# One core: where the row scales are fetched, and the order of loads and scalings between block 0 and block 1 of a layer norm, state-space and Mish kernel

## The chip, the cores and the metric

The kernel runs on one core of a Trainium2 chip. Its time is the device time of one execution in microseconds. A profile is one execution recorded by the hardware profiler; its span runs from the first to the last instruction.

## The reference

x is 2048 rows of 1024 numbers (bf16). It is normalised by rows, and two branches of the normalised rows are added to x:

```
xn  = layernorm(x)
B_bar = ((exp(dt*Lambda) - 1) / Lambda)[:, None] * (B_re + 1j*B_im)
Bu  = xn @ B_bar.T                       # 1024 complex states
h_t = exp(dt*Lambda) * h_(t-1) + Bu_t    # along the 2048 rows
A   = 2 * real(h @ C.T) + xn * Dskip
hh  = xn @ w1 + b1                       # 1024 -> 3584
B   = (hh * tanh(softplus(hh))) @ w2     # Mish, 3584 -> 1024
out = x + A + B
```

## The kernel before, in words

**Blocks.** The rows are worked in four blocks of 512. For each block the kernel computes w1 and Mish (28 tiles of 128 columns, `first_tile`), the projection into the states (B), the recurrence on VectorE (`recur`, state chunks j = 0 to 7), the product with w2 (`dense`) and the projection out of the states (C), which adds up in the same PSUM banks as w2; `finish` then adds the banks to x, and `store` writes x out on ScalarE's queue. Block 0 uses plain products. From block 1 on, the product with B and most of that with w1 are done in a fast form: seven products of half size per 2 by 2 partition (numbers 1 to 7), for which sums and differences of the factors are needed, in f16. For that the factors must first be scaled by powers of two.

**What is prepared during block 0's tail for block 1.** (1) *B*: `rows_load(i)` reads 16 row chunks of B (eight buffers within `act`, given by `row_slot`) on GpSimd's queue; `rows_size(i)` on ScalarE sums their absolute values and at its end issues load i + 8; `rows_scale(h)` on VectorE makes the scales of half h (states 0 to 511 for h = 0, from sizes 0 to 7) and stores them as a row to DRAM (`scd`); `rows_fetch(h)` reads that row back, spread over 128 partitions, to act buffer 18 + h; `rows_spread(h)` puts it in order and `scale_B` multiplies B by it on VectorE. (2) *w1*: seven groups of 512 columns. `w_load(i)` reads a group raw, four DMAs on GpSimd's queue (group 3 to hb buffers 8 to 15, group 4 to hb 0 to 7, group 5 to act 20 to 27); `w_scale(i)` scales it on ScalarE, two instructions, and stores three quarters of it (`wsd`) on GpSimd's queue; `w_sums(i)` makes the four sums on VectorE and stores these. SyncE's ring loads bring the stored units back as they are used. (3) *C*: `scale_C(j)` scales C on ScalarE and VectorE with scratch in hb 0 to 7; `keep_C(j)` stores it on ScalarE's queue.

**What sets the order.** Each engine works its instructions in the order in which the program emits them, its DMA issues among them; there is no planner. An instruction waits by semaphores for the last writer of what it reads, and for the last writer and all readers of what it writes; a buffer that is only named among the writes orders instructions in the same way:

```python
        waits = _hazards(reads, writes, ev)
        self.items.append((fn, waits.values(), dsem.sem, 16))
        _record(reads, writes, ev)
```

PSUM has eight banks; block 1's tiles 0 to 11 use bank f % 8, and a bank is free again when ScalarE's Mish of its tile has read it. Block 0's last additions (`finish`, q = 0 to 3) free banks 0 and 1, then 2 and 3, and so on. Block 0's w2 items are used in the order 0 to 8, 13, 9 to 12 (item g covers act buffers 2g and 2g + 1), so buffers 18 and 19 are read by the eleventh item and 20 and 21 by the twelfth.

At the start of block 1 (`side(0)`), VectorE makes the sums of B (`sums_B`) and of x (`sums_x`, written over block 0's x, once that is stored), then the sums of groups 3 and 4. Block 1's products (L952 with B, L1024 with w1) follow in the order written in `WHOLE`; `w_load(6)` waits until group 3's hb buffers have been stored.

Of the kernel before, what the change touches and what calls it, by code (L numbers as in the profile page):

```python
# [142 lines left out]
def bass_parallel_sum__ssm_conv_s5__dense_activation_mish__prompt_kernel(  # L143
    nc: bass.Bass,
    A_x: bass.AP,
    A_Lambda_re: bass.AP,
    A_Lambda_im: bass.AP,
    A_B_re: bass.AP,
    A_B_im: bass.AP,
    A_C_re: bass.AP,  # L150
    A_C_im: bass.AP,
    A_log_dt: bass.AP,
    A_Dskip: bass.AP,
    B_x: bass.AP,
    B_w1: bass.AP,
    B_b1: bass.AP,
    B_w2: bass.AP,
    out: bass.AP,
):
    build_kernel(nc, A_x, A_Lambda_re, A_Lambda_im, A_B_re, A_B_im, A_C_re, A_C_im,  # L160
                 A_log_dt, A_Dskip, B_w1, B_b1, B_w2, out)


def build_kernel(nc, A_x, A_Lambda_re, A_Lambda_im, A_B_re, A_B_im, A_C_re, A_C_im,
# [5 lines left out]
    TB = 512  # L170
# [44 lines left out]
    AC = Queue(nc, "ac")  # L215
    PO = Queue(nc, "po")
    SP = Queue(nc, "sp")
# [15 lines left out]
    b_actf = [Buf("act%d" % f, parts=[Buf("act%d_%d" % (f, h)) for h in range(2)]) for f in range(NF)]  # L233
# [45 lines left out]
    def c(n):  # L279
        return cs[:, CN.index(n), :]  # L280
# [28 lines left out]
    srow0 = act[:, 18:20, :].rearrange("p f t -> p (f t)")  # L309
# [9 lines left out]
    def wsm(n, lo, hi):  # L319
        return cs[:, CN.index("den") + n, lo:hi]  # L320
# [759 lines left out]
    def w_unit(where):  # L1080
        kind, t = where
        v = hb if kind == "h" else act
        return v[:, t:t + 2, :].rearrange("p f t -> p (f t)"), (b_hbf if kind == "h" else b_actf)[t:t + 2]
# [3 lines left out]
    def w_raw(i, ci, kh):  # L1087
        kind, t = W_RAW[i]
        return kind, t + 2 * (2 * ci + kh)

    def w_load(i):
        sem = DmaSem(nc, "d_wraw%d" % i, nper=4)
        for ci in range(2):
            for kh in range(2):
                dst, b_dst = w_unit(w_raw(i, ci, kh))
                f0 = (4 * i + 2 * ci) * P
                src = B_w1[kh * NH * P:(kh + 1) * NH * P, f0:f0 + 2 * P].rearrange("(k p) f -> p k f", p=P)
                PO.dma(lambda e, dst=dst, src=src: e.dma_start(dst.rearrange("p (k f) -> p k f", k=NH), src),
                       sem, writes=b_dst)

    def w_half(i, ci):
        kind, t = w_raw(i, ci, 0)
        v, b_v = (hb, b_hbf) if kind == "h" else (act, b_actf)
        return v[:, t:t + 4, :].rearrange("p f t -> p (f t)"), b_v[t:t + 4]
# [53 lines left out]
    def w_store(i, n, t, b_t):  # L1158
        PO.dma(lambda e: e.dma_start(wsd[i][n - 1], t), DmaSem(nc, "d_wsd%d_%d" % (i, n)),  # L1159
               reads=b_t, writes=[b_wsd[i][n - 1]])  # L1160

    def w_scale(i, cis=(0, 1)):
        for ci in cis:
            t, b_t = w_half(i, ci)
            aop(lambda e, t=t: e.activation(t, t, AF.Copy, scale=wsm(2, i, i + 1)),  # L1165
                reads=b_t + [b_wsm[2][i]], writes=b_t)
        for n, ci, kh in ((1, 0, 0), (2, 0, 1), (4, 1, 1)):
            if ci in cis:
                w_store(i, n, *w_unit(w_raw(i, ci, kh)))
# [288 lines left out]
    def carry(queue=VE):  # L1458

        hl = hT[:, :, :, TB - 1]  # L1460
        for s, n in enumerate(("c1", "s1")):
            for ci in range(2):
                o = qi[:, ci, :] if s == 0 else qt[:, ci, :]
                queue.op(lambda e, o=o, n=n, ci=ci: e.tensor_tensor(o, hl[:, ci, :], c(n), op=ALU.mult),
                    reads=b_hT[ci] + [b_cs[n]], writes=[b_qi if s == 0 else b_qt[ci]])
        queue.op(lambda e: e.tensor_tensor(qi[:, 0, :], qi[:, 0, :], qt[:, 1, :], op=ALU.subtract),
            reads=[b_qi, b_qt[1]], writes=[b_qi])
        queue.op(lambda e: e.tensor_tensor(qi[:, 1, :], qi[:, 1, :], qt[:, 0, :], op=ALU.add),
            reads=[b_qi, b_qt[0]], writes=[b_qi])
# [253 lines left out]
    NHS = 8  # L1723
# [3 lines left out]
    def row_slot(i):  # L1727
        f0 = (12, 0, 2, 4, 6, 8, 10, 14)[i % NHS]
        return act[:, f0:f0 + 2, :].rearrange("p f t -> p (f t)"), b_actf[f0:f0 + 2]

    def rows_load(i):
        j, ci = i // 2, i % 2
        t, b_t = row_slot(i)
        if NHS // 2 <= i < NHS:
            b_t = b_t + [b_actf[19]]
        PO.dma(lambda e: e.dma_start(t, (A_B_re, A_B_im)[ci][j * P:(j + 1) * P, :]), s_nat[i % NHS], writes=b_t)

    def rows_size(i):
        j, ci = i // 2, i % 2
        t, b_t = row_slot(i)  # L1740
        aop(lambda e: e.activation(t, t, AF.Abs, scale=2.0, accum_out=cj("ab%d" % ci, j)), reads=b_t,  # L1741
            writes=b_t + [b_ab[ci][j // 4]])
        if i + NHS < 2 * NJ:
            rows_load(i + NHS)

    def rows_scale(h):
        hs = slice(NJ // 2 * h, NJ // 2 * (h + 1))
        ab0, ab1, ss, si = (c(n)[:, hs] for n in ("ab0", "ab1", "ss", "si"))
        e8, f8 = si_i[:, 0, hs], si_i[:, 1, hs]
        b_a, b_e, b_f = b_ab[0][h], b_si_i[0][h], b_si_i[1][h]  # L1750

        def power(o, b_o, src, b_s, m, a):
            vop(lambda e: e.tensor_scalar(f8, src, m, a, op0=ALU.mult, op1=ALU.add), reads=[b_s], writes=[b_f])
            vop(lambda e: e.tensor_scalar(o.bitcast(i32), f8, 23, None, op0=ALU.logical_shift_left), reads=[b_f], writes=[b_o])

        vop(lambda e: e.tensor_tensor(ab0, ab0, ab1, op=ALU.add), reads=[b_a, b_ab[1][h]], writes=[b_a])
        vop(lambda e: e.tensor_scalar(ab0, ab0, 2.0 ** 100, 2.0 ** -100, op0=ALU.min, op1=ALU.max),
            reads=[b_a], writes=[b_a])
        vop(lambda e: e.tensor_scalar(e8, ab0.bitcast(i32), 24, None, op0=ALU.logical_shift_right),
            reads=[b_a], writes=[b_e])  # L1760
        power(ss, b_ss[h], e8, b_e, -2.0, 2.0 * 127 + 9)
        vop(lambda e: e.tensor_copy(sbf[:, hs], ss), reads=[b_ss[h]], writes=[b_sbf[h]])
        power(si, b_si[h], e8, b_e, 1.0, 59.0)
        power(ab1, b_ab[1][h], e8, b_e, -1.0, 195.0)
        (AC if h else PO).dma(lambda e: e.dma_start(scd[h], sbf[:, hs]), DmaSem(nc, "d_scd%d" % h),
                              reads=[b_sbf[h]], writes=[b_scd[h]])

    def rows_fetch(h):
        (AC if h else PO).dma(lambda e: e.dma_start(srow0[:, TB * h:TB * (h + 1)],
                                     scd[h].rearrange("p j -> (p j)").partition_broadcast(P)),  # L1770
               DmaSem(nc, "d_srow%d" % h), reads=[b_scd[h]], writes=[b_actf[18 + h]])

    def rows_spread(h):
        vop(lambda e: e.tensor_copy(srow[:, TB * h:TB * (h + 1)].rearrange("p (j q) -> p j q", q=P),
                                    srow0[:, TB * h:TB * (h + 1)].rearrange("p (q j) -> p j q", q=P)),
            reads=[b_actf[18 + h]], writes=[b_actf[16 + h]])

    def keep_C(j):
        AC.dma(lambda e: e.dma_start(ctd[j], CT[:, j, :, :].rearrange("p c d -> p (c d)")), s_ctd[j],
               reads=[b_CT[j]], writes=[b_ctd[j]])  # L1780
# [5 lines left out]
    def scale_B(pr, cis=(0, 1)):  # L1786
        js = slice(2 * pr, 2 * pr + 2)
        b_B = b_BT[js]
        row = srow[:, 2 * P * pr:2 * P * (pr + 1)].rearrange("p (j q) -> p j q", j=2)
        for ci in cis:  # L1790
            vop(lambda e, ci=ci: e.tensor_tensor(
                BT[:, ci, js, :, :], BT[:, ci, js, :, :], row.unsqueeze(2).to_broadcast([P, 2, NK, P]), op=ALU.mult),
                reads=b_B + [b_actf[16 + pr // 2]], writes=b_B)
# [29 lines left out]
    for blk in range(NB):  # L1823
# [67 lines left out]
        for j in range(NJ):  # L1891
# [49 lines left out]
            if j == 3:  # L1941
                for i in range(NHS):
                    rows_load(i)
# [15 lines left out]
                w_sums(i, True)  # L1959
        if blk == FAST - 1:  # L1960
            keep_C(NJ - 1)
            w_load(4)
            w_load(5)
            rows_scale(1)
            for n in ("c1", "s1"):
                PO.op(lambda e, n=n: e.tensor_tensor(c(n), c(n), c("ab1"), op=ALU.mult), reads=[b_cs[n]] + b_ab[1], writes=[b_cs[n]])
            carry(PO)
            rows_fetch(1)
        for _ in out_stage:
            pass  # L1970
        if blk == FAST - 1:
            w_scale(3)
            w_scale(4)
            rows_spread(0)
            scale_B(0)
            scale_B(1, (0,))
# [36 lines left out]
```

## Time and profile before

| | us |
|---|---|
| three runs | 597.64, 598.75, 594.12 |
| median | 597.64 |
| profiled execution: time | 599.66 |
| profiled execution: span | 598.4 |
| busy: TensorE / VectorE / ScalarE / GpSimd | 587.6 / 504.8 / 402.8 / 156.4 |

The profile's lines name engine, source line and operation, and the tiles as out<-in. In a timeline a row gives start and duration in us, the number of instructions merged in it, and in brackets the idle time of the engine before it with what ended it. A q behind an engine's name is its sequencer, which issues DMAs. In a table of stages each engine's busy time and number of instructions are followed by the granted TensorE clock (1.00 is full), the share of the DMA engines' time, and GB/s. Matmuls overlap: 128 x 512 ones start 0.216 us apart, though each is drawn with 0.38 us.

### The profile page before, as it was taken

To read this page: it belongs to the slowest core of one execution; us is meant where nothing else is said; L and a number is where in the kernel's file an instruction comes from. 1 tells how busy PE (TensorE), PEld (TensorE's weight loads), DVE (VectorE), ACT (ScalarE), POOL (GpSimd) and SP (SyncE) were. 2 spreads that over 40 slices of the span, in tenths; PEclk is the share of its full clock that TensorE was granted. 3 is DMA by queue.
4 is the path that set the end of the run, shared out by engine and by line. 5 is a ranking of instruction groups with operands and counts; after the bars stand their busy time and mean duration, and the time that the engine had idled before them with its cause. 6 is when DMAs were issued, how large, how long until landed. Compare 5 with 4: busy or idle time off the path is not lost.

```text
span 598.4 us, 9801 instructions
## 1 busy us (share of the span) xinstructions
PE 587.6 (98%) x3643; PEld 355.2 (59%) x3643; DVE 504.8 (84%) x759; ACT 402.8 (67%) x540; POOL 156.4 (26%) x221
## 2 busy tenths in 40 slices
PE   9999999999887999999999999999999999999998
PEld 8644444444333888544448888744446888854444
DVE  6998896997697868999765869899999468789995
ACT  4879981765649977899805677889621798893330
POOL 2899300103645421341210321011510013100000
PEclk9999999999997999999999999999999999999999
DMA  8999999998688989798969967979995956989831
GB/s 252 292 231 244 153 191 213 271 384 286 184 267 297 348 304 332 268 326 236 271 244 403 338 214 254 300 242 276 315 334 187 392 183 219 339 319 321 294 125 70
DMA packets 115785, 160.32 MB, mean 268 GB/s; under 512 B 56074, under 2 KB 67082, under 8 KB 115738
## 3 DMA queue, kind: packets, MB, share of 16 engines
q1 hardware_dynamic: 97696, 105.99, 59.9%
q0 software_dynamic: 13520, 44.19, 23.0%
q10 hardware_dynamic: 4522, 9.52, 4.3%
q8 instruction: 29, 0.48, 0.3%
q14 instruction: 18, 0.15, 0.1%
HBM read 113.52 MB, written 34.08 MB: 247 GB/s over the span
## 4 chain that ended last, share of the span: by engine, by line
PE 88%; DMA 6%; ACT 3%; DVE 2%; issue 1%; ACTq 0%; DVEq 0%; POOLq 0%
PE ps L1484 33%; PE ps L1024 17%; PE ps L952 12%; PE ps L1543 9%; PE ps L875 8%; PE ps L1420 5%; DMA act<-in_A_B_im_dram 2%; DMA ring<-wsd 2%; DMA act<-in_A_B_re_dram 2%; ACT hb L1165 1%; PE ps L684 1%; PE ps L693 1%; ACT act L1741 1%; DVE xx L1683 1%; PE ps L646 1%
## 5 line engine op out<-in xcount | busy, mean ns | idle before, releaser
L1484 PE MATMUL ps<-ring,act 128*128 128x512 bf16 x608 | 131.9, 379 | 0.0
L1484 PEld LDWEIGHTS ps<-ring,act 128*128 128x128 bf16 x608 | 59.5, 98 | 71.3
L1044 ACT ACTIVATE snaps<-ps,par,cs 128x256 f32<-128x256 f32 x98 | 53.4, 563 | 58.2 <-PE ps L1024 36.0
L1484 PE MATMUL ps<-ring,hT 128*128 128x512 bf16 x362 | 78.6, 379 | 0.0
L1024 PE MATMUL ps<-TT,ring 128*128 128x256 f16 x576 | 71.1, 273 | 0.1
L914 DVE TENSOR_TENSOR mt<-hT,tab 128x2048 bf16<-128x2048 bf16 (+1 forms) x56 | 67.9, 1213 | 0.4
L875 PE MATMUL ps<-xnT,ring 128*128 128x512 bf16 x264 | 59.8, 389 | 7.5 <-ACT act L883 5.6
L1024 PEld LDWEIGHTS ps<-TT,ring 128*128 128x128 f16 (+1 forms) x576 | 56.1, 98 | 7.8 <-DMA ring<-wsd 0.3
L1484 PEld LDWEIGHTS ps<-ring,hT 128*128 128x128 bf16 x362 | 35.4, 98 | 42.8
L1435 DVE TENSOR_TENSOR_SCAN hT<-cs,qi,hT 128x512 bf16<-128x512 f32 x48 | 60.7, 1275 | 0.0
L1061 DVE SCALAR_TENSOR_TENSOR act<-ps,cs,snaps 128x512 bf16<-128x512 f32 x54 | 39.8, 748 | 18.8 <-PE ps L1024 16.7
L1024 PE MATMUL ps<-xnT,ring 128*128 128x256 bf16 x432 | 54.5, 273 | 0.0
L875 PEld LDWEIGHTS ps<-xnT,ring 128*128 128x128 bf16 x264 | 26.2, 100 | 40.6 <-issue 11.5
L1209 POOL DMA_DIRECT2D w2d<-hb x28 | 20.1, 718 | 97.3 <-ACT hb L1219 53.7
L1024 PEld LDWEIGHTS ps<-xnT,ring 128*128 128x128 bf16 (+1 forms) x432 | 42.3, 98 | 5.3
L977 DVE TENSOR_TENSOR hT<-ps,snaps 128x512 f16<-128x512 f32 x36 | 23.8, 686 | 15.0 <-ACT snaps L969 13.7
L1455 ACT ACTIVATE hT<-hT,wz 128x1024 bf16<-128x1024 bf16 x16 | 17.9, 1144 | 27.4 <-DVE hT L1450 27.4
L898 ACT ACTIVATE act<-act 128x2048 bf16<-128x2048 bf16 (+3 forms) x12 | 32.8, 2756 | 4.7 <-DVE act L1047 4.7
L1159 POOL DMA_DIRECT2D wsd<-hb x35 | 19.0, 546 | 43.9 <-DVE hb L1181 28.0
L1543 PE MATMUL ps<-ring,act 128*128 128x512 bf16 (+1 forms) x132 | 29.8, 379 | 0.0
L1165 ACT ACTIVATE hb<-hb,cs 128x2048 bf16<-128x2048 bf16 x10 | 19.3, 1993 | 13.8 <-DVE SS L1804 13.8
L1420 PE MATMUL ps<-xnT,BT 128*128 128x512 bf16 x128 | 27.8, 379 | 0.0
(236 smaller groups left out, 1056.3 us busy)
## 6 DMA issues: line engine op xcount, KB each, us to landing
ring<-wsd SPq DMA_DIRECT2D x126, 256.0 KB, 5.3
ring<-in_B_w_dram SPq DMA_DIRECT2D x58, 512.0 KB, 5.4
ring<-ctd SPq DMA_DIRECT2D x24, 512.0 KB, 5.6
ring<-w2d SPq DMA_DIRECT2D x24, 512.0 KB, 5.1
wsd<-hb POOLq DMA_DIRECT2D x35, 256.0 KB, 5.0
w2d<-hb POOLq DMA_DIRECT2D x28, 256.0 KB, 5.0
hb<-in_B_w_dram POOLq DMA_DIRECT2D x20, 256.0 KB, 5.3
ctd<-CT ACTq DMA_DIRECT2D x8, 512.0 KB, 5.9
```

Source lines behind the costliest of these rows:

```text
L875: PE.mm(lambda e, k=k, w=w: e.matmul(ps[:, bank, :], lhsT=w, rhs=xnT[:, k, :], start=k == 0, stop=k == NK - 1), reads=[b_ring[s]] + b_xnT, ...
L898: aop(lambda e: e.activation(t, t, AF.Mish), reads=b, writes=b)
L914: vop(lambda e: e.tensor_tensor(mt[:], u.unsqueeze(1).to_broadcast([P, 2, 2, TB]), tab[:, :, j, :].unsqueeze(2).to_broadcast([P, 2, 2, TB] ...
L952: PE.mm(lambda e, w=w, x=x, o=o, begin=begin, end=end: e.matmul(ps[:, bank, o:o + TH], lhsT=w, rhs=x, start=opens and begin, stop=end, ski ...
L1024: PE.mm(lambda e, w=w, x=x, o=o, begin=begin, end=end: e.matmul(ps[:, bank, o:o + TH], lhsT=w, rhs=x, start=opens and begin, stop=end, ski ...
L1044: aop(lambda e, o=o, p=p, j=j: e.activation(o, p, AF.Identity, scale=ig, bias=b1(f0 + j)), reads=[b_ps[b], b_par, b_ig], writes=b_dst)
L1061: vop(lambda e: e.scalar_tensor_tensor(out=dst, in0=bank(b), scalar=ig, in1=src, op0=ALU.mult, op1=ALU.add), reads=[b_ps[b], b_snap[k], b_ ...
L1165: aop(lambda e, t=t: e.activation(t, t, AF.Copy, scale=wsm(2, i, i + 1)), reads=b_t + [b_wsm[2][i]], writes=b_t)
L1420: PE.mm(lambda e, j=j, ci=ci, k=k, bank=bank: e.matmul(ps[:, bank + ci, :], lhsT=BT[:, ci, j, k, :], rhs=xnT[:, k, :], start=k == 0, stop= ...
L1435: vop(lambda e: e.tensor_tensor_scan(out=hT[:, ci, j, :], data0=cj("r", j).to_broadcast([P, TB]), data1=hT[:, ci, j, :], initial=init, op0 ...
L1484: PE.mm(lambda e: e.matmul(ps[:, u, :], lhsT=lhsT, rhs=rhs, start=st_, stop=last, skip_group_check=blk in SPLIT), reads=reads, writes=[b_p ...
L1543: PE.mm(lambda e: e.matmul(ps[:, bank, :], lhsT=lhsT, rhs=rhs, start=st_, stop=end, skip_group_check=True), reads=b_t + [b_ring[s]], write ...
```

## The change

Five edits, all at the end of block 0:

- `rows_load`: before, each of loads 4 to 7 names act buffer 19 among its writes; after, load 4 alone names act buffer 21.
- `rows_fetch`: the fetch of half 0 moves from GpSimd's queue, that of half 1 from ScalarE's, to SyncE's.
- `rows_scale(1)` and `rows_fetch(1)` are emitted ahead of `w_load(4)`.
- `w_load(5)` is emitted after GpSimd's small products and the carry in place of before them.
- `w_scale(3)` is emitted before the rest of block 0's output stage (the last projection, the additions and the x stores) in place of after it.

```diff
     def rows_load(i):
         j, ci = i // 2, i % 2
         t, b_t = row_slot(i)
-        if NHS // 2 <= i < NHS:
-            b_t = b_t + [b_actf[19]]
+        if i == NHS // 2:
+            b_t = b_t + [b_actf[21]]
         PO.dma(lambda e: e.dma_start(t, (A_B_re, A_B_im)[ci][j * P:(j + 1) * P, :]), s_nat[i % NHS], writes=b_t)
...
     def rows_fetch(h):
-        (AC if h else PO).dma(lambda e: e.dma_start(srow0[:, TB * h:TB * (h + 1)],
+        SP.dma(lambda e: e.dma_start(srow0[:, TB * h:TB * (h + 1)],
                                      scd[h].rearrange("p j -> (p j)").partition_broadcast(P)),
                DmaSem(nc, "d_srow%d" % h), reads=[b_scd[h]], writes=[b_actf[18 + h]])
...
         if blk == FAST - 1:
             keep_C(NJ - 1)
+            rows_scale(1)
+            rows_fetch(1)
             w_load(4)
-            w_load(5)
-            rows_scale(1)
             for n in ("c1", "s1"):
                 PO.op(lambda e, n=n: e.tensor_tensor(c(n), c(n), c("ab1"), op=ALU.mult), reads=[b_cs[n]] + b_ab[1], writes=[b_cs[n]])
             carry(PO)
-            rows_fetch(1)
+            w_load(5)
+            w_scale(3)
         for _ in out_stage:
             pass
         if blk == FAST - 1:
-            w_scale(3)
             w_scale(4)
             rows_spread(0)
             scale_B(0)
```

## The prediction

> **What bounds the kernel now.** I read the page first, then TensorE's timeline around the one dip in its row of slices, then the timelines of ScalarE, GpSimd, VectorE and SyncE over the same 60 us, following each wait to what released it.
>
> ```profile
> PE 587.6 (98%) x3643; PEld 355.2 (59%) x3643; DVE 504.8 (84%) x759; ACT 402.8 (67%) x540; POOL 156.4 (26%) x221
> ...
> 145.84 15.49 PE L1484 MATMUL ps<-CT,hT 128*128 128x512 bf16 x71
> 163.15 13.97 PE L875 MATMUL ps<-xnT,ring 128*128 128x512 bf16 x64 [1.83 <-DVE xx L1683]
> 182.75 9.37 PE L875 MATMUL ps<-xnT,ring 128*128 128x512 bf16 x32 [5.63 <-ACT act L883]
> ...
> 163.00:175.50 12.50, 12.35 (x58) 5.65 (x59) 11.45 (x14) 2.57 (x2) 6.42 (x13) 1.00 0.92 281
> 182.70:186.00 3.30, 3.25 (x8) 1.17 (x9) 3.10 (x5) 3.30 (x5) 1.21 (x3) 0.50 0.94 312
> ```
>
> TensorE is busy for 587.6 of 598.4 us, so at most 10.8 us can come from waits; 1.83 + 5.63 = 7.46 us of them stand here, where block 0 ends and block 1 begins. The stages view adds a third loss: the granted clock is 1.00 after the short wait and 0.50 after the long one. At full clock 64 matmuls of this shape take 13.97 us, starting 0.216 us apart, so 32 should take 6.91; they took 9.37. Lost in this place: 1.83 + 5.63 + 2.46 = 9.92 us.
>
> The long wait is for the first Mish of block 1, which must empty PSUM bank 0. ScalarE shows why it is late:
>
> ```profile
> 141.00 1.06 ACT L1741 ACTIVATE act<-act 128x1024 bf16<-128x1024 bf16 x1 [2.86 <-DMA act<-in_A_B_re_dram]
> 147.55 1.06 ACT L1741 ACTIVATE act<-act 128x1024 bf16<-128x1024 bf16 x1 [3.31 <-DMA act<-in_A_B_im_dram]
> ...
> 158.90 0.18 ACT L1741 ACTIVATION_READ_ACCUMULATOR act<-act 128x1 f32 x1
> 160.96 0.33 ACTq L1765 DMA_DIRECT2D scd<-sbf  x1
> 170.17 0.33 ACTq L1769 DMA_DIRECT2D act<-scd  x1
> 170.53 2.35 ACTq L1669 DMA_DIRECT2D out_dram<-xx  x4
> 172.93 7.68 ACT L1165 ACTIVATE hb<-hb,cs 128x2048 bf16<-128x2048 bf16 x4 [13.84 <-DVE SS L1804]
> 180.63 1.28 ACT L883 ACT_TABLE_LOAD   x1
> ```
>
> The 13.84 us are put down to VectorE, but the issue column tells it better: ScalarE's queue issues the store of the second half's row scale at 160.96 and then its fetch (L1769), which cannot go before the store has landed, at 170.17. Everything behind it stands still: four stores of x, four scalings of w1 groups 3 and 4 (7.68 us), the table load, Mish.
>
> GpSimd shows the other half of the story:
>
> ```profile
> 123.89 0.54 POOL L1736 DMA_DIRECT2D act<-in_A_B_re_dram  x1 [11.49 <-PE ps L1484]
> 129.72 0.54 POOL L1736 DMA_DIRECT2D act<-in_A_B_im_dram  x1 [5.29 <-DMA act<-in_A_B_re_dram]
> 136.30 0.54 POOL L1736 DMA_DIRECT2D act<-in_A_B_re_dram  x1 [6.04 <-DMA act<-in_A_B_im_dram]
> 141.26 0.54 POOL L1736 DMA_DIRECT2D act<-in_A_B_im_dram  x1 [4.43 <-DMA act<-in_A_B_re_dram]
> ...
> 150.21 0.55 POOL L1765 DMA_DIRECT2D scd<-sbf  x1 [0.68 <-DVE cs L1754]
> 155.92 0.54 POOL L1769 DMA_DIRECT2D act<-scd  x1 [5.17 <-DMA scd<-sbf]
> 156.45 5.96 POOL L1098 DMA_DIRECT2D hb<-in_B_w_dram  x8
> 162.40 2.97 POOL L1098 DMA_DIRECT2D act<-in_B_w_dram  x4
> ...
> 168.23 1.18 POOL L1468 TENSOR_TENSOR qi<-qi,qt 128x8 f32<-128x8 f32 x1
> ...
> 188.41 2.99 POOL L1098 DMA_DIRECT2D hb<-in_B_w_dram  x4 [4.13 <-DMA wsd<-hb]
> ...
> DMA to landing us min/median/max: 4.6/7.0/9.5
> ```
>
> (The last row is the issue to landing, shortest, median and longest, of the twelve raw w1 loads issued from 156.45.) Row loads 4 to 7 of B run one at a time, each waiting for the landing of the one before: all four name act buffer 19 among their writes, so each is a second writer of it. These landings are ScalarE's two waits of 2.86 and 3.31 us above, and through ScalarE VectorE's:
>
> ```profile
> 144.27 1.28 DVE L837 SCALAR_TENSOR_TENSOR CT<-CT,cs,ct 128x1024 bf16<-128x1024 bf16 x1 [0.95 <-ACT ct L836]
> 148.73 0.16 DVE L1756 TENSOR_TENSOR cs<-cs 128x4 f32<-128x4 f32 x1 [1.86 <-ACT act L1741]
> 159.12 0.16 DVE L1756 TENSOR_TENSOR cs<-cs 128x4 f32<-128x4 f32 x1 [2.59 <-ACT act L1741]
> 161.78 4.61 DVE L1683 TENSOR_TENSOR xx<-ps,xx 128x1024 bf16<-128x1024 f32 x4
> 175.26 0.69 DVE L1811 TENSOR_TENSOR TT<-xnT 128x1024 f16<-128x1024 bf16 x1 [0.74 <-DMA out_dram<-xx]
> 189.10 2.48 DVE L1791 TENSOR_TENSOR BT<-BT,act 128x2048 bf16<-128x2048 bf16 x2
> 194.58 0.69 DVE L977 TENSOR_TENSOR hT<-ps,snaps 128x512 f16<-128x512 f32 x1 [3.01 <-ACT snaps L969]
> 196.97 0.69 DVE L977 TENSOR_TENSOR hT<-ps,snaps 128x512 f16<-128x512 f32 x1 [1.70 <-ACT snaps L969]
> 202.27 1.28 DVE L977 TENSOR_TENSOR hT<-ps,snaps 128x512 f16<-128x512 f32 x2
> ```
>
> Its four additions that end block 0 (L1683) start at 161.78, after the second half's row scale; TensorE's short wait is for the first of them.
>
> **The change, part by part.**
>
> *Row loads.* Only load 4 waits, for act buffer 21 in place of 19: one w2 item later on TensorE, 16 matmuls of 0.216 us = 3.45 us. So load 4 issues at 127.3 and 5, 6, 7 right behind, the last at 129.0. The landings read off above took 5.3 to 6.3 us; load 7 lands by about 135.5, twelve us earlier. ScalarE loses both waits, 6.17 us: its last row size ends at 152.9 in place of 159.1. The later loads (8 to 15) wait on GpSimd only for sizes that now come earlier.
>
> *First half's scale.* VectorE's idle 0.95 and 1.86 go: the scale starts at 145.9 in place of 148.7, its store on GpSimd at 147.4. The fetch leaves GpSimd's queue, and with it 5.17 + 0.54 us ahead of the raw w1 loads: group 3's four (0.75 us each) issue from 147.9 to 150.9 and land, by the row of their landings, at 155 to 160.4. Group 4's wait for the last scaling of C on VectorE, which I put at 152.4 (145.9, the scale 1.85, the last rotation 2.0, two scalings 2.6); they issue until 155.4 and land at 160 to 164.9. They pass the second half's scale in the program, but this is stored from ScalarE, so nothing on GpSimd stands between.
>
> *Second half's scale.* It starts when ScalarE's sizes end, 153.0, and takes 2.8 us as before. VectorE is then free at 155.8, before TensorE's first output row is complete: the projection ends at 161.3, its four groups 0.86 us apart, the first at 158.7. The additions run 158.8 to 163.4 and the first ends near 159.9, before TensorE needs the bank at 161.3. **The 1.83 us go.**
>
> *ScalarE.* The store of the second scale goes near 154.9, the fetch is SyncE's. Group 3's scaling (two of 1.92 us) runs from 155.3 to 159.1, in time that was a wait, and ahead of the x stores; if its load lands last, at 160.4, it ends at 162.3. The x stores follow the additions, the last at 163.9; group 4's scaling ends at 167.9, table load and first Mish (0.84 with the hand-over) at 170.0; with the latest landings 171. TensorE needs bank 0 again after eight tiles, at 161.3 + 64 x 0.216 = 175.1. **The 5.63 us go, with 4 to 5 us in hand**, and with no long wait the half clock too, 2.46 us. Sum: -9.92 us.
>
> The Trainium skill (TensorE: Matmul & The Clock Gate, What's actually happening) says that half clock comes after an idle window of some 3.4 us and lasts until some 3.4 us of work have passed; the 0.50 after 5.63 us and the 1.00 after 1.83 agree. By its figure the slow stretch would cost an estimated 1.7 us and the sum would be -9.2.
>
> *SyncE.* It takes both fetches. Its timeline has a hole there:
>
> ```profile
> 113.58 17.10 SPq L462 DMA_DIRECT2D ring<-in_B_w_dram  x9
> 177.64 26.24 SPq L459 DMA_DIRECT2D ring<-wsd  x15
> ```
>
> From 130.7 to 177.6 it issues nothing. The first fetch goes when its store has landed (5.4 us after issue before, so 153) and is used at 163.4; the second store took 9.2 us, so 164, plus a landing like the w1 loads' 4.6 to 9.5: 174 at the latest, for a use on VectorE near 179.7. Queued behind it is only the first load of scaled w1, which TensorE wants near 192.5 (now two products, 1.75 us, before the 204.19 below). Cost nothing; without that hole each us would delay ring loads.
>
> *Group 5 and the carry.* The carry (4.0 us from 165.4 to the end of L1468) starts when the second scale is done, 155.9; group 5's loads follow from 160 to 163, no later than their 162.40 before, and group 3's stores behind them at 163, twelve us ahead of now. Cost nothing.
>
> *What is late next.* TensorE comes 9.9 us earlier to block 1's products. VectorE's preparation moves only by 3.0 (the additions end at 163.4, not 166.4) and the 0.74 wait for x stores, which now land in time: 3.7 us. It is 6.2 us later against TensorE than now. Its idle 3.01 and 1.70 us take up 4.7; 1.5 remain at the two joins of 202.27, which end at 202.9 and 203.55 and whose banks TensorE takes up at 204.19 and 205.06:
>
> ```profile
> 204.19 1.91 PE L952 MATMUL ps<-TT,BT 128*128 128x256 f16 x16
> 212.92 1.91 PE L1024 MATMUL ps<-TT,ring 128*128 128x256 f16 x16
> ...
> L459 SPq DMA_DIRECT2D ring<-wsd x5: 320/454/732, 197.3 to 199.3; - x5
> ...
> DMA to landing us min/median/max: 4.8/5.6/6.7
> ```
>
> The slack is 1.3 us, so a new wait of 0.2 us, between 0 and 4.9 (none of VectorE's idle usable). The second product chain is the scaled w1: group 4's sums are stored behind GpSimd's wait at 188.41, itself for the landing of group 3's. The last of the five loads that depend on them went at 199.3, landed by 206.0 and was used for the second product from 212.92, at 213.8: 7.8 us in hand, 6.2 needed. Taken as 0; at most 2.1 if that chain does not move at all.
>
> **Sum:** -9.92 + 0.2 = -9.7 us, 589.9 for the profiled execution (599.66, span 598.4). The median of the three runs is 597.64, 2.0 below it; I forecast **588.0** for a median.
>
> **Rivals.** (a) *VectorE or the w1 stores become the bound in block 1.* For it: lost slack of 6.2 us against 1.3 + 4.7 and 7.8. Against it: both still fit, just. Times: 2.1 us lost for the stores alone gives 590, 4.9 for VectorE 592.6, both nearly 595. Chance 0.18.
>
> (b) *The row loads don't come earlier*, since seven to eleven of them meet the w1 ring loads in full DMA queues. Then ScalarE's sizes end at 159 and the 1.83 us stay, but the fetch still leaves ScalarE: group 3 scales from 161.3, the x stores end near 167.5, group 4 at 171.4, the first Mish at 173.5, before the 176.9 at which TensorE then needs the bank. Gain 8.1, time 589.6. Against it: the loads of 141.26 to 145 were eight in a row and ScalarE did not wait again. Chance 0.09.
>
> (c) *Slower: VectorE holds up GpSimd's issues.* The raw loads of groups 3 and 4 now issue among VectorE's long scalings and rotations, up to 1.28 us each. If each issue has to let two such instructions pass (0.75 + 2.56 = 3.3 us), eight issues run from 147.9 to 174.3; group 4 lands at 178.9, its last scaling ends at 180.8 and the first Mish at 182.9: a wait of 7.8 us and the half clock, as much as is lost now. That is the point from which it decides; at three instructions each (4.6 us) Mish ends at 193, 18 us late, and the time is about 608. Against it: row loads at 141.26 and after took 0.54 us each beside a busy VectorE. The Trainium skill (SBUF — State Buffer, SBUF: two separate sides) describes this lock and has a 0.62 us issue grow to 3.1 us beside a VectorE copy, an estimate at the break-even point; the 0.54 speak against it. Chance 0.04.
>
> **How the numbers follow.** The forecast (gain 8.5 to 10) has 0.69, the rivals as given. Its own range is 587 to 590 with the 0.4% by which runs differ: 585 to 591. To hold eight in ten I reach to (a): 585 to 594. A measurement here tells about 1%, 6 us, from no change, so faster needs a time under 591.7: the forecast, (b) and most of (a), less some for what I missed: 0.85; within 1%: 0.10; slower: 0.05.
>
> **What would show it.** Right: four row loads 0.54 us apart near 127; no fetch on ScalarE or GpSimd; w1 scaling on ScalarE before the x stores, near 155; TensorE without a wait over 1 us from 145 to 200 and no stage at clock 0.50; block 1's products from 182. Wrong: a Mish wait left before 185, raw w1 issues over 1 us each, or a wait at the products over 2 us.

## The result, and the profile after

The changed kernel takes 593.15 us (median of 22 runs, 591.88 to 600.66), the kernel before 597.75 (22 runs, 591.11 to 606.24): a ratio of 0.9944, 95% interval 0.9919 to 0.9968. The interval lies wholly below 1, so the kernel is faster, but by 4.6 us and not by 9.6. The forecast of 588.0 is missed, and so is the line that the prediction drew for "faster" (under 591.7): by it the result lies in the class "within 1%", which had a chance of 0.10. It falls inside the range of 585 to 594 only because that range was stretched to take in rival (a); the forecast's own range ended at 591. The profiled execution took 594.85 us, its span is 593.6.

Runs over 1.5% above the fastest of their kernel are left out of the ratios but stand in the medians and ranges; e6, e10, e11 and e12 below make several such runs, and they are named there.

TensorE's busy line and its timeline after, with two stages of it. In a stage, the columns are each engine's busy time and instructions, the granted clock, the DMA share and GB/s.

```profile
PE 586.5 (99%) x3643; PEld 355.1 (60%) x3643; DVE 504.3 (85%) x759; ACT 403.1 (68%) x540; POOL 153.2 (26%) x220
...
162.18 20.88 PE L875 MATMUL ps<-xnT,ring 128*128 128x512 bf16 x96
182.90 3.66 PE L952 MATMUL ps<-xnT,BT 128*128 128x256 bf16 x32
...
206.66 3.21 PE L1024 MATMUL ps<-TT,ring 128*128 128x256 f16 x16 [2.57 <-DMA ring<-wsd]
...
284.63 27.79 PE L1484 MATMUL ps<-ring,hT 128*128 128x512 bf16 x128
...
175.00:180.00 5.00, 5.00 (x25) 2.27 (x24) 4.79 (x9) 4.83 (x8) 1.07 (x2) 1.00 0.03 12
207.10:210.50 3.40, 3.40 (x18) 2.35 (x16) 1.35 (x2) 0.00 (x0) 0.00 (x0) 0.50 1.00 376
```

The rows of the kernel before that stand against these, where they were not shown yet:

```profile
191.96 3.66 PE L952 MATMUL ps<-xnT,BT 128*128 128x256 bf16 x32
...
289.21 27.79 PE L1484 MATMUL ps<-ring,hT 128*128 128x512 bf16 x128
...
175.00:180.00 5.00, 2.12 (x10) 0.78 (x8) 4.60 (x8) 5.00 (x3) 2.66 (x5) 1.00 0.67 226
```

The dip where block 1 begins is gone: 96 matmuls in one unbroken row of 20.88 us where two rows (64 and 32 matmuls), two waits and a stretch at clock 0.50 stood. The first product comes at 182.90 against 191.96, though this execution was 1.0 us behind as it entered block 0's last stages. Up to there the gain is 10.1 us, more than the 9.92 expected. From there on it shrinks: first product to the first projection out of `hT` takes 284.63 - 182.90 = 101.73 us, before 289.21 - 191.96 = 97.25. The 4.48 us lost again lie in one place, 206.66: a wait of 2.57 us for a ring load of scaled w1, 3.4 us at clock 0.50 behind it (1.7 lost), 0.2 elsewhere. ScalarE and GpSimd after:

```profile
151.60 0.19 ACT L1741 ACTIVATION_READ_ACCUMULATOR act<-act 128x1 f32 x1
153.03 0.33 ACTq L1765 DMA_DIRECT2D scd<-sbf  x1
154.73 3.90 ACT L1165 ACTIVATE hb<-hb,cs 128x2048 bf16<-128x2048 bf16 x2 [2.95 <-DMA hb<-in_B_w_dram]
161.04 3.73 ACTq L1669 DMA_DIRECT2D out_dram<-xx  x4
164.82 3.89 ACT L1165 ACTIVATE hb<-hb,cs 128x2048 bf16<-128x2048 bf16 x2 [6.20 <-DVE act L1774]
...
170.03 1.26 ACT L883 ACTIVATE act<-ps,par 128x512 bf16<-128x512 f32 x2
```

```profile
128.37 0.54 POOL L1736 DMA_DIRECT2D act<-in_A_B_re_dram  x1 [14.94 <-ACT act L1741]
...
129.94 0.54 POOL L1736 DMA_DIRECT2D act<-in_A_B_im_dram  x1
...
144.64 0.54 POOL L1765 DMA_DIRECT2D scd<-sbf  x1 [2.42 <-DVE cs L1754]
145.18 3.00 POOL L1098 DMA_DIRECT2D hb<-in_B_w_dram  x4
...
155.25 0.20 POOL L1468 TENSOR_TENSOR qi<-qi,qt 128x8 f32<-128x8 f32 x1
...
193.98 1.07 POOL L1159 DMA_DIRECT2D wsd<-hb  x2 [2.32 <-ACT hb L1165]
...
196.40 2.99 POOL L1098 DMA_DIRECT2D hb<-in_B_w_dram  x4
```

No fetch is left on either queue. The four row loads lie 0.53 us apart, the last size ends at 151.79 (152.9 forecast), the scaling of w1 group 3 stands ahead of the x stores, and Mish starts at 170.03 in place of 181.9. The last two rows hold what goes wrong later: two of the stores of scaled w1 (a third follows them), and the raw load of w1 group 0 (`n0` in `WHOLE`, four DMAs of 256 KB). Before, the same stores and raw loads issued 9.1 us later:

```profile
203.04 1.08 POOL L1159 DMA_DIRECT2D wsd<-hb  x2 [2.32 <-ACT hb L1165]
...
205.47 3.00 POOL L1098 DMA_DIRECT2D hb<-in_B_w_dram  x4
```

They follow ScalarE's scaling and moved with it. The ring load that TensorE waits for at 206.66 hangs on VectorE's sums and moved from 199.3 to 195.7 only (its rows are below, at e3). So before it was under way for 3.7 us when these stores set in, and had all but landed when the raw loads came; after, two of the three stores stand right ahead of it, the third right behind, and the raw loads follow within 0.7 us.

### The profile page after: what moved, and what is told of

The parts are those of the page before. It is cut to its first block, busy times and chain, and to the rows that moved or that the text cites. A ratio compares the mean times of both kernels' runs of the same rounds, so it can differ in the third digit from the quotient of the medians.

```text
span 593.6 us, 9801 instructions
## 1 busy us (share of the span) xinstructions
PE 586.5 (99%) x3643; PEld 355.1 (60%) x3643; DVE 504.3 (85%) x759; ACT 403.1 (68%) x540; POOL 153.2 (26%) x220
## 4 chain that ended last, share of the span: by engine, by line
PE 90%; DMA 5%; ACT 2%; SPq 1%; DVE 1%; POOL 1%; issue 0%; ACTq 0%
PE ps L1484 39%; PE ps L1024 17%; PE ps L952 10%; PE ps L1543 9%; PE ps L875 6%; PE ps L1420 5%; DMA ring<-wsd 2%; DMA wsd<-hb 1%; DMA ring<-in_B_w_dram 1%; PE ps L693 1%; DVE xx L1683 1%; ACT tab L1783 1%; ACT hb L1165 1%; SPq L459 1%; ACT act L883 1%; PE ps L1507 1%
## 5 line engine op out<-in xcount | busy, mean ns | idle before, releaser
L1024 PE MATMUL ps<-TT,ring 128*128 128x256 f16 x576 | 72.4, 276 | 2.6 <-DMA ring<-wsd 2.6
L875 PE MATMUL ps<-xnT,ring 128*128 128x512 bf16 x264 | 57.3, 379 | 0.0
L1484 PE MATMUL ps<-CT,hT 128*128 128x512 bf16 x128 | 27.8, 379 | 0.0
```

Of the source, the lines that this page charges most:

```text
L875: PE.mm(lambda e, k=k, w=w: e.matmul(ps[:, bank, :], lhsT=w, rhs=xnT[:, k, :], start=k == 0, stop=k == NK - 1), reads=[b_ring[s]] + b_xnT, ...
L1024: PE.mm(lambda e, w=w, x=x, o=o, begin=begin, end=end: e.matmul(ps[:, bank, o:o + TH], lhsT=w, rhs=x, start=opens and begin, stop=end, ski ...
L1484: PE.mm(lambda e: e.matmul(ps[:, u, :], lhsT=lhsT, rhs=rhs, start=st_, stop=last, skip_group_check=blk in SPLIT), reads=reads, writes=[b_p ...
```

## The experiments

Twelve kernels in three groups (e1 to e4, e5 to e8, e9 to e12), each group on one chip beside the kernel before (medians 599.09, 598.11 and 597.77 us there). In this table the two stages are read off TensorE's timeline of the profiled execution as above: the twelve w1 tiles that open block 1, and first product to first `hT` projection. Ratios are to the kernel before on the same chip; e6's rests on nine runs and e10's on four. e11 and e12 stand in the text only.

| kernel | median us (runs) | ratio, 95% | w1 tiles | products | its largest waits |
|---|---|---|---|---|---|
| before | 597.75 (22) | 1 | 28.81 | 97.25 | 1.83, 5.63 in block 1 |
| after | 593.15 (22) | 0.9944 [0.9919, 0.9968] | 20.72 | 101.73 | 2.57 |
| e1 | 592.27 (6) | 0.9893 [0.9853, 0.9933] | 20.72 | 99.48 | 2.54 in block 0, 1.66 |
| e2 | 594.70 (6) | 0.9940 [0.9895, 0.9984] | 20.72 | 103.76 | 0.82, 1.15, 2.34 |
| e3 | 592.51 (6) | 0.9907 [0.9867, 0.9946] | 20.72 | 99.30 | 0.76, 0.75 |
| e4 | 591.02 (6) | 0.9868 [0.9836, 0.9900] | 20.72 | 99.06 | 0.51, 0.39, 1.07 |
| e5 | 592.92 (12) | 0.9939 [0.9906, 0.9972] | 20.72 | 97.33 | 3.22 in block 0 |
| e6 | 593.45 (12) | 0.9928 [0.9894, 0.9962] | 20.72 | 99.27 | 9.84 in block 0 |
| e7 | 592.73 (12) | 0.9943 [0.9913, 0.9972] | 20.72 | 99.42 | 1.33 |
| e8 | 595.80 (12) | 0.9961 [0.9918, 1.0003] | 20.72 | 103.28 | 4.19 |
| e9 | 598.90 (12) | 1.0009 [0.9976, 1.0042] | 24.44 | 98.25 | 3.56 |
| e10 | 590.00 (6) | 0.9873 [0.9830, 0.9917] | 20.72 | 97.32 | none over 0.3 |

**e1: the row loads alone.** The kernel before, with the first hunk of the diff and nothing else.

```diff
-        if NHS // 2 <= i < NHS:
-            b_t = b_t + [b_actf[19]]
+        if i == NHS // 2:
+            b_t = b_t + [b_actf[21]]
```

> The kernel before with the one edit in the row loads (load 4 alone waits, for act buffer 21); fetches, raw loads and the scaling of group 3 stay as before. Theory A (the row loads were the root of both waits): ScalarE's sizes end near 152, the second scale's store goes at 153, its fetch at about 161.5, group 3 and 4 are scaled from 165 to 172.6, the first Mish ends near 174.6, before TensorE needs the bank at 175.2. Both waits at the start of block 1 are gone and the time is that of the full change, 592 to 594 us. Rival B (the fetch on ScalarE's queue was the root): the wait for the first Mish stays, 2 us or more, and the time is 595 us or more.

592.27 us: the one index carries as much as the whole change (593.15). Its profiled execution lost time in two other places, both waits for ring loads:

```profile
126.16 12.22 PE L1484 MATMUL ps<-ring,act 128*128 128x512 bf16 x48 [2.54 <-DMA ring<-in_B_w_dram]
...
209.43 1.92 PE L1024 MATMUL ps<-TT,ring 128*128 128x256 f16 x16 [1.66 <-DMA ring<-wsd]
```

The second is the changed kernel's wait again, so it comes with the earlier start and not with SyncE's fetches. The first is in block 0, ahead of everything that was edited. In their profiled executions e2 (0.32 us), e4 (0.51), e5 (3.22), e6 (9.84) and e7 (0.72) wait in block 0 for w2 ring loads too. e7 is the changed kernel itself, whose first profile shows no such wait, so this wait comes and goes between executions of one kernel.

**e2: everything but the row loads.** The change, with that hunk undone.

> The full change without its edit in the row loads (loads 4 to 7 each name act buffer 19, as before). Theory A: the 1.8 us wait for the first addition comes back, the first Mish ends near 173.5 and TensorE does not wait for it; block 1's products start near 184; the wait for scaled w1 in them is 2 us or more because VectorE's preparation does not move. Time 593 to 596 us. Rival B: the same as the full change, 592 to 594 us, with no wait before the products.

594.70, on one chip with e1 (592.27): by the medians the queue edits alone gain less, but the two intervals overlap, so the times alone do not settle it. The trace says more. Its Mish is in time, but its row sizes are late as in the kernel before, so VectorE ends block 0 late (0.82 us for the first addition) and the products lose most of all, 103.76:

```profile
162.93 20.88 PE L875 MATMUL ps<-xnT,ring 128*128 128x512 bf16 x96 [0.82 <-DVE xx L1683]
...
209.44 3.41 PE L1024 MATMUL ps<-TT,ring 128*128 128x256 f16 x16 [2.34 <-DMA ring<-wsd]
```

Either half removes the Mish wait in the profile; in the times they do not add.

**e3: the raw loads moved away.** `n0`, the raw load of w1 group 0 on GpSimd's queue, is emitted behind the products p7 and q7 in place of before p1. These are the four DMAs that issue at 196.40 in the change, 0.7 us behind the ring load that comes late; the stores of scaled w1 stay.

```diff
-    WHOLE = "... P1 Q0 n0 p1 q1 ... q3 p7 q7 k0 ..."
+    WHOLE = "... P1 Q0 p1 q1 ... q3 p7 q7 n0 k0 ..."
```

> The full change with the raw load of w1 group 0 (1 MB, four DMAs on GpSimd's queue) emitted after the products p7 q7 in place of before p1. Theory C (what ate half the gain is DMA traffic that now meets in one place: the ring load for p7 q7 took 10.9 us to land where it took 6.7 before): with 1 MB less in the queues it lands in 7 to 9 us, the wait of 2.6 us shrinks below 1 us and no stage falls to half clock; time 589 to 590.5 us. Theory D (the load was issued too late, since the stores of the group 4 sums hang on VectorE, which moved by 4 us only): the wait stays above 2 us, time 592.5 to 594 us.

592.51. In its profiled execution the raw loads issue at 201.89, and the wait for the scaled w1 is gone. Two waits come later, for ring loads of w2, which landed in 7.3 to 9.8 us here against 3.8 to 5.9 in the change; the moved raw loads now lie nearer to them, but why they are slower was not tested.

```profile
201.89 3.00 POOL L1098 DMA_DIRECT2D hb<-in_B_w_dram  x4
...
230.70 0.61 PE L1484 MATMUL ps<-ring,act 128*128 128x512 bf16 x2 [0.76 <-DMA ring<-in_B_w_dram]
232.05 0.60 PE L1484 MATMUL ps<-ring,act 128*128 128x512 bf16 x2 [0.75 <-DMA ring<-in_B_w_dram]
```

The load that the changed kernel waits for was followed through four kernels. First before, then after, then e3, then e4: duration of the issue in ns and its start, and time from issue to landing. The row of e4 holds two loads; the second, issued at 188.0, is the one in question, and it landed after 7.4 us.

```profile
L459 SPq DMA_DIRECT2D ring<-wsd x1: 732/732/732, 199.3 to 199.3; - x1
...
DMA to landing us min/median/max: 6.7/6.7/6.7
```

```profile
L459 SPq DMA_DIRECT2D ring<-wsd x1: 1027/1027/1027, 195.7 to 195.7; - x1
...
DMA to landing us min/median/max: 10.9/10.9/10.9
```

```profile
L459 SPq DMA_DIRECT2D ring<-wsd x1: 658/658/658, 194.3 to 194.3; - x1
...
DMA to landing us min/median/max: 8.6/8.6/8.6
```

```profile
L459 SPq DMA_DIRECT2D ring<-wsd x2: 377/408/438, 187.6 to 188.0; - x2
...
DMA to landing us min/median/max: 6.9/7.1/7.4
```

Measured from the first product, the issue moved from 7.4 us (199.3 - 191.96) to 12.8 (195.7 - 182.90), 5.4 us later, and the landing grew by 4.2. TensorE takes the tile 20.96 us after its first product (212.92 - 191.96), when before it had been there 6.9 us: 5.4 + 4.2 - 6.9 = 2.7, and 2.57 were measured. In e3 the load landed at 202.9, 0.1 us ahead of its matmuls: it issued about as long after the first product as in the change (12.3 us against 12.8) and landed in 8.6 us in place of 10.9. The raw loads are all that e3 moves. In the traces in which they issue within 1 us of this load, it lands in 10.0 to 10.9 us (after, e1, e2, and e7, which is the change once more), so 1.5 to 2.3 of the 4.2 us by which the landing grew go with them.

What the DMA engines did while this load was under way, before and after (the last two columns are their busy share and GB/s):

```profile
199.30:206.00 6.70, 6.70 (x64) 6.00 (x62) 6.40 (x18) 6.67 (x8) 2.69 (x5) 1.00 0.99 381
...
195.70:206.60 10.90, 8.39 (x77) 7.27 (x75) 9.39 (x22) 8.10 (x15) 5.72 (x9) 1.00 1.02 345
```

They were full both times. Rate times duration gives an estimate of 2.5 MB moved before and 3.8 MB after, and 3.1 MB in e3 (366 GB/s over 8.6 us): the load had more to share the engines with. The other 1.9 us or more, with the stores of scaled w1 beside it still, were not taken apart.

**e4 and e5: w1's sums first.** Both let VectorE sum groups 3 and 4 (`w_sums`) before block 1's x sums; e4 puts them ahead of both halves of B's; e5 puts group 3's there and group 4's between. The edit, shortened, as e5 has it, with e4's place marked:

```diff
     scale_B(1, (1,))
+    w_sums(3)
+    w_load(6)
     sums_B(0)
+    w_sums(4)           # e5: here; e4: one line up, ahead of sums_B(0)
     # the four x sums, then sums_B(1)
-    w_sums(3)
-    w_load(6)
     rows_spread(1)
     scale_B(2)
-    w_sums(4)
     scale_B(3)
```

> The full change with the sums of w1 groups 3 and 4 (and the raw load of group 6 between them) put ahead of the sums of B and x on VectorE at the start of block 1. Theory D: the group 4 sums are stored 5 us or more earlier, the ring loads are issued 4 to 8 us earlier, and TensorE does not wait in block 1's products: 588 to 590 us, the 9.7 us that were forecast. Theory C alone: the loads still land slowly, but the lead is larger than the 2.6 us, so the wait goes as well; the landings of the ring loads near 195 to 207 stay at 8 us or more. If the time stays at 592 to 594 although the wait at p7 q7 is gone, the loss lies elsewhere.

e4: 591.02, all six runs between 589.89 and 592.39. The same load issues 7.7 us earlier and lands in 7.4 us. VectorE is now late with B instead, for 0.39 and 1.07 us:

```profile
184.98 1.92 PE L952 MATMUL ps<-xnT,BT 128*128 128x256 bf16 x16 [0.39 <-DVE BT L1804]
...
196.71 1.92 PE L952 MATMUL ps<-TT,BT 128*128 128x256 f16 x16 [1.07 <-DVE hT L977]
```

> The full change with the group 3 sums ahead of the sums of B, and the group 4 sums between the sums of the first and of the second pair of B (ahead of those of x). In e4 VectorE stood 1.6 us for the landing of group 4's raw stores, and TensorE then 1.1 and 0.4 us for VectorE. Theory D (what ate half the gain is the late issue of the ring loads behind VectorE's chain): neither wait is left, block 1 from its first product to its C projection takes 97.5 us (97.25 before, 101.7 in the full change, 99.1 in e4), time 589 to 590.5 us. If that stretch stays at 99 or more, something else than the sums' place holds TensorE there.

e5: its products take 97.33 us against 97.25 before, so 4.4 of the 4.48 us are back in this execution. Yet its median is 592.92 over twelve runs, from 589.62 to 599.20. Five lie under 591.4; the profiled one, of span 593.5, lost its time in block 0, with 3.4 us of half clock behind the wait:

```profile
126.76 11.96 PE L1484 MATMUL ps<-ring,act 128*128 128x512 bf16 x47 [3.22 <-DMA ring<-in_B_w_dram]
```

**e6: no gate at all.** The change, with no extra buffer named by any row load.

```diff
-        if i == NHS // 2:
-            b_t = b_t + [b_actf[21]]
```

> The full change with no load of B held back (load 4 names no other buffer). Theory E (the gate only keeps 1 MB of row loads out of the way of the w2 ring loads that block 0 still needs): loads 4 to 7 go at 113 to 115, the ring loads for block 0's last w2 items land 2 to 4 us later, TensorE waits 1 to 3 us near 120 to 130, and the time is 1 to 4 us above the full change, 594 to 597. Rival F (the gate does nothing any more): as the full change, 592 to 594, without a wait there.

Nine of twelve runs lie at 591.93 to 598.1, like the change; three take 604, among them the profiled one. In that one all eight row loads issue at 110.2 to 114.1, among block 0's last w2 ring loads. The source view of these ring loads shows how late they landed; in the change the longest of them took 12.1 us:

```profile
133.32 5.05 PE L1484 MATMUL ps<-ring,act 128*128 128x512 bf16 x16 [9.84 <-DMA ring<-in_B_w_dram]
...
L462 SPq DMA_DIRECT2D ring<-in_B_w_dram x11: 378/553/14197, 100.4 to 129.3; - x11
...
DMA to landing us min/median/max: 4.7/22.7/28.9
```

So the remaining gate buys no speed in most executions. That it keeps the slow ones away is likely but not shown: three of twelve runs are slow here and none of twelve in e7, the change on the same chip, but e5, which has the gate, also had ring loads of w2 that landed only after 16.8 us.

**e7 and e9: the change and the kernel before once more**, unchanged, each on the chip of its group.

> The full change once more, for its waits and its time beside the others of this group: 592 to 594 us; the wait at p7 q7 of 1.5 to 3 us again, with or without a half clock behind it.

> The kernel before, unchanged, for a second profile of it. The forecast took the whole 9.9 us of one execution, whose time was 2 us above the median. Theory H (that loss is not the same in every execution, because it hangs on how long single DMAs take to land): the wait for the first Mish is another length here, by 1 us or more, and the half clock may be missing; ScalarE's scale store lands in another time than 9.2 us. Rival: the same waits of 1.8 and 5.6 us within 0.5.

e7 repeats the ratio: 0.9943. Its profiled execution waits for the same ring load, but 1.33 us and without a slow clock:

```profile
205.02 1.92 PE L1024 MATMUL ps<-TT,ring 128*128 128x256 f16 x16 [1.33 <-DMA ring<-wsd]
```

e9 is what the forecast lacked: the kernel before in another execution, of time 594.08 and span 592.9, which lies 3.7 us below the median where the prediction's lay 2.0 above its own. Mish again starts behind the fetch on ScalarE's queue, but the store landed in 7.9 us (158.01 to 165.87; 9.2 in the execution the prediction used), the wait is 3.56 us, and no half clock follows: 32 matmuls take 7.07 us, where 9.37 stood. The wait of 1.83 us is absent too; one of 0.54 follows. So the stage of twelve w1 tiles takes 24.44 us and not 28.81. The store's landing accounts for 1.3 of the 2.1 us by which the long wait is shorter.

```profile
158.01 0.33 ACTq L1765 DMA_DIRECT2D scd<-sbf  x1
...
165.87 0.33 ACTq L1769 DMA_DIRECT2D act<-scd  x1
...
178.49 7.07 PE L875 MATMUL ps<-xnT,ring 128*128 128x512 bf16 x32 [3.56 <-ACT act L883]
```

**e8: row loads and e5's order, without the queue edits.** Is the small version enough?

```diff
 # the kernel before, with
+        if i == NHS // 2:
+            b_t = b_t + [b_actf[21]]
 # and w_sums(3), w_load(6), w_sums(4) placed as in e5
```

> The kernel before with two edits: the row loads of the change and the order of sums of e5; fetches, raw loads and scaling as before. Theory A (the row loads alone carry what the change brings): as e5 within 1 us, 589 to 591.5. Rival G (the other edits matter once block 1 no longer waits): 1.5 us or more above e5, through later row scales and group 4 scaling.

By the medians no: 595.80 against 592.92 for e5 on the same chip; but the intervals overlap, and it is the trace that tells them apart. ScalarE scales groups 3 and 4 only behind the x stores here, so VectorE, which now takes the sums early, finds the w1 not ready, stands 5.44 us, and hands that on to TensorE as 4.19 us with a slow clock behind it:

```profile
163.63 7.68 ACT L1165 ACTIVATE hb<-hb,cs 128x2048 bf16<-128x2048 bf16 x4 [12.29 <-DVE act L1774]
```

```profile
174.00 2.87 DVE L1181 TENSOR_TENSOR hb<-hb 128x1024 f16<-128x1024 bf16 x4 [5.44 <-DMA wsd<-hb]
```

```profile
187.80 2.58 PE L952 MATMUL ps<-xnT,BT 128*128 128x256 bf16 x16 [4.19 <-DVE BT L1804]
```

So the queue edits earn their place here: they have the w1 scaled in time for the earlier sums.

**e10 to e12: later transposes.** The late ring loads of block 0 issue on SyncE behind the DMA transposes of block 1's x. These kernels start the transposes later: e10 in e5, e11 in the kernel before, e12 in the change.

```diff
-            at = (17, 19, 21, 23) if blk else (5, 6, 7, 8)
+            at = (17, 19, 21, 23) if blk else (13, 15, 17, 19)
```

> The kernel of e5 with the four transposes of block 1's x on SyncE's queue emitted four w2 items and more later in block 0, so that block 0's last w2 ring loads are issued ahead of them. Theory I (the scatter of several us, and the 3.2 us wait at 127 in e5, come from w2 ring loads that wait on SyncE behind a transpose that waits for VectorE): no wait in block 0's w2 product, all but one or two of its runs within 589 to 591.5, median 590. Rival: the loads are late for lack of bandwidth alone; the wait stays in some executions and the median is 592 to 593.5 as in e5.

> The kernel before with the transposes moved as in e10 and nothing else. Theory I: its runs scatter less; the waits at the start of block 1 stay, so 595 to 599 us.

> The full change with the transposes moved as in e10, the sums as in the change. Theory I: 591.5 to 592.5 us with little scatter, 1.5 to 2.5 above e10 by the wait at p7 q7 that is left; beside e11 this is the size of the change without the scatter of block 0: 4 to 7 us.

Half of it holds. Four of e10's six runs take 589.74 to 590.17 us, matched here only by e4's best three (589.89 to 590.01); the profiled one, of span 588.9, has no wait over 0.3 us in these stages. The other two take 604.5 and 620.0. e11 (median 604.87, eight of twelve runs at 604.5 and above; ratio 1.0056 [1.0014, 1.0098] over seven runs) and e12 (611.26 over all its runs, 591.63 to 630.93, ten of thirteen at 607 and above; ratio 0.9955 [0.9892, 1.0018] over the other three) are mostly like those. e12's source view of the transposes, and the rows in which its profiled execution (span 628.2) loses most:

```profile
L624 SPq DMA_TRANSPOSE xnT<-xn x14: 1242/2386/15466, 7.0 to 449.3; - x14
...
DMA to landing us min/median/max: 3.3/7.4/35.3
```

```profile
172.10 1.06 ACT L1741 ACTIVATE act<-act 128x1024 bf16<-128x1024 bf16 x1 [15.37 <-DMA act<-in_A_B_re_dram]
...
178.44 0.16 DVE L1756 TENSOR_TENSOR cs<-cs 128x4 f32<-128x4 f32 x1 [20.10 <-ACT act L1741]
...
181.58 17.04 PE L875 MATMUL ps<-xnT,ring 128*128 128x512 bf16 x68 [19.48 <-DVE xx L1683]
```

TensorE's 19.48 us are not a wait for a transpose's result. They go back through VectorE's first addition and a row size on ScalarE to a row load of B that took 27.2 us to land. The DMA engines tell more: from 160 to 170 us, with transposes under way, their busy share is 1.15 and they move 125 GB/s; e10's good execution moves 371 there at a share of 1.03. e5 shows the same on a small scale: 127 GB/s at a share of 1.02 from 115 to 120 us with a transpose under way, 397 in the 5 us after. So while a transpose is late, other transfers seem to be late with it; this is read from the times and not tested. The place is a bad one for this cure. What makes some executions of e10 good and others not is open.

## Why the prediction was right about the place and wrong about the gain

**Right: the mechanism and the place.** Row sizes, both scales, the scaling of w1 and Mish come within some 3 us of the times written down, in the order written down. The waits of 1.83 and 5.63 us and the slow stretch are gone. Every sign that the prediction wrote down for "right" came, from the row loads 0.53 us apart to a first product at 182.90; of its signs for "wrong", a wait at the products over 2 us came as well. The value of the path was about right too: e10, which frees it and loses nothing later, has a span of 588.9, 9.5 us below the 598.4 from which 9.9 were to go (it carries e5's order and the later transposes beside the change, so it is no pure measure).

**Wrong: the step "what is late next".** It said that the last scaled w1 load had "7.8 us in hand, 6.2 needed. Taken as 0; at most 2.1". The runs showed 4.48 us lost there, of 10.1 gained: a wait of 2.57 us and 1.7 us of half clock behind it. The shift was somewhat over, at 6.2 (5.4 to 5.5 by the trace). Two things beside it were not well sized:

- The slack was counted to the load's own use, the second half of the ring item. Both halves count on one semaphore, so the first half's matmuls, at 212.92, wait for both landings: 6.9 us in hand. (The same slip stands in the prediction's "if its load lands last, at 160.4, it ends at 162.3": a group's four raw loads count on one semaphore too, so both scalings would wait. It cost nothing.)
- The landing was kept at 6.7 us. It took 10.9 after, and 7.4 in e4, where it issues 7.7 us earlier. ScalarE's w1 stores and the raw loads behind them moved 9.1 us ahead with TensorE, this load 3.6 with VectorE, and so they met. From 175 to 180 us the DMA engines moved 12 GB/s, where before they moved 226; when the load went, they were full. e3, which takes the raw loads away and nothing else, lowers the landing to 8.6 and the wait is gone; e4, which issues ahead of the crowd, lowers it to 7.4; e5 and e10 issue early too and have no wait there. So the meeting is shown as the cause of this wait, with the raw loads at 1.5 to 2.3 of the 4.2 us; that the stores make up the rest was read from the times.

At 2.57 us the wait lies beyond the bound of 2.1, which held no term for landing; with it came a slow clock, 1.7 us, which the sum had at none. Rival (a) named this place and the size of 2.1, and had 0.18; it gave as the reason a chain that does not move, not a longer landing. That the time fell in the range is owed to it. It should have been the forecast's own term: 1.6 us of slack (7.8 - 6.2) was less than the 4.2 us by which the landing grew. The other term there, 0.2 us for `a4`/`b4`, was fair: 195.18 - 182.90 is 12.28 us, before 204.19 - 191.96 = 12.23.

**Wrong: the base.** All 9.9 us of one execution were taken off a median that lay 2.0 us below that execution. e9 shows what it hides: a loss that swings with the landing of one small store, and a slow clock in one execution and not in the other. A median run of before lies 597.75 - 589.8 = 7.9 us above e10's undisturbed four, so 7.9 us is about what it had to lose, as far as these four stand for the kernel without waits (they carry two edits more). The balance: 9.7 forecast = 4.6 measured + 1.8 of base + about 2.4 for the wait at the products in a common run (592.2 against 589.8) + 0.9 from that to the median. The 2.4 are borne out by e7's trace, of an execution of 592.15 us: its products take 2.1 us more than e10's, and it waits 0.72 in block 0. The 0.9 are a remainder, read from the spread of runs.

**The other rivals.** (b) fell: the loads came early. (c) fell as clearly: four raw w1 loads take 3.00 us to issue, 0.75 each, beside a busy VectorE, in every kernel. Cover that was claimed and held: SyncE's hole took both fetches, and its first scaled-w1 load went at 165.52, before 177.64. The carry took 1.7 us (153.77 to 155.45).

## What to carry to other kernels

When one engine's wait is removed, list what hangs on the engines that did not move as far; give each transfer among them not only its shift but a longer landing, since the traffic of two stages closes up, and count slack to the first use of anything that shares a semaphore with it. Take a gain from several executions of the kernel before: the long wait in one profile may be the worse end of a wait that swings. And edits that do not add up (e1, e2) may still be needed for the next one (e5 against e8).

## What was not expected of the hardware

**The slow clock does not follow the length of a wait.** Waits of 2.34 (e2), 2.54 (e1), 2.57 (after), 3.22 (e5) and 4.19 us (e8) each brought 3.4 us at 0.50; the 5.63 us brought 6.8, of which the first 2.1 lay in the wait itself; 1.33 (e7), 1.83 and even 3.56 us (e9) brought none. The Trainium skill (TensorE: Matmul & The Clock Gate, What's actually happening) has the activity counted in free-running windows of 3.4 us; the multiples of 3.4 agree, and such a window's phase would account for a 3.56 that goes free, but hardly for a 2.34 that does not.

**Landing times stretch several fold under load.** The 512 KB ring loads of one stage land in 4.7 us or 28.9 (e6), DMA transposes in 3.3 us or 35.3 (e12). The run times scatter between executions of one kernel as if such landings changed from one to the next, but few kernels here have two traces to show it.
